# A clustered-attention, soft-MoE and PReLU kernel: the feed-forward's first steps in another order, another dispatch of the second batch, one more weight unit fetched in attention

## The chip, the cores and the metric

The kernel runs on one core of a Trainium2 chip. The metric is the device time of one execution in microseconds; three executions of the kernel before were timed, and one more was profiled.

## The reference

Three layers stand one behind the other, in float32. Attention has 2 batches of 8 heads, 768 tokens and 64 features: each query and key is assigned to one of 16 centroids of its head, and a query sees only the keys of its own cluster. The result, 1536 tokens of 512 features, goes through a soft mixture of 8 experts with 4 slots each, and then through a feed-forward with PReLU.

```python
mask = q_assign[:, :, :, None] == k_assign[:, :, None, :]
scores = np.where(mask, scale * np.matmul(q, k.transpose(0, 1, 3, 2)), -1e9)
attn = np.exp(scores - np.max(scores, axis=-1, keepdims=True))
x = np.matmul(attn / (np.sum(attn, axis=-1, keepdims=True) + 1e-09), v)   # then (1536, 512)
logits = x @ phi                                                          # (1536, 32)
d = np.exp(logits - logits.max(0, keepdims=True)); d /= d.sum(0, keepdims=True) + 1e-09
slot_input = (d.T @ x).reshape(E, S_per_e, D)
slot_out[e] = np.maximum(slot_input[e] @ w1[e], 0.0) @ w2[e]              # for each expert e
c = np.exp(logits - logits.max(1, keepdims=True)); c /= c.sum(1, keepdims=True) + 1e-09
h = (c @ slot_out) @ w_in                                                 # d_ff = 2048
out = (np.maximum(h, 0.0) + alpha * np.minimum(h, 0.0)) @ w_out
```

## The kernel before

The order of the instructions on each engine is the order in which the program issues them; nothing re-orders them later. In attention that order comes from a table. Every step of every head is an event with a due time, `add(key, step, ...)`, where a head has six units of time, `s0 = 6 * h`; the events are sorted by their due times and each is issued as soon as the steps that it needs have been issued. The due times are entries of `TABLE`. Its field `ha` holds counts of filler matmuls of the start (`heat`: products that nobody reads), `hb`, `hn` and `wk` those of other places, and `w` the list of expert weights that are fetched while attention runs.

Weights come in units of 1 MiB. Each expert has four, two of `w1` and two of `w2`, so there are 32. Nineteen of them are fetched in attention, into a ring of 18 tiles (`r`, the pool `wr`, which the operands of the heads share) and into the tiles of attention's operands as these come free (`a`, `b`, `c`). After attention three more go into the pool `we`, and the others follow as the experts release the ring (`more_w`). All these transfers, and the heads' operands, are issued by one engine, SP (SyncE), in program order; an entry of that queue that has to wait for its tile holds those behind it.

The feed-forward's weights are words of 64 bits that are turned into float32 high and low parts on the chip. `w_in` is prepared in attention (`win_word`, `win_bits`, `win_sum`, `win_store`): its first 512 columns stay in the chip, and three quarters go to DRAM and come back with `win_back(1)` to `win_back(3)` on the same queue. `w_out` is loaded by `load_o` and prepared in the feed-forward.

After the last head come, in program order: the dispatch of the second batch (`dispatch(1, 0)` to `dispatch(1, 2)`: maximum over the tokens for each slot, exponential, sums, the product with the tokens), the slots' inputs `siT`, eight experts with the combination's steps `comb_step` between, and the slot outputs `so`, `sob`, `soT`. There is one factor for each batch, because each batch had a maximum of its own.

The feed-forward begins with the string `ff` of `TABLE`. Each word is a step: `W0` to `W3` are 16 matmuls each that multiply the slot outputs by a quarter of w_in (`w_prime`; W0 is written to the PSUM tile `Wq`, W1 to W3 to `Wr`), `p0` to `p3` split the first 128 columns of W0's result into high and low part (`w_base`), and `c1` copies the rest out of `Wr` (`take`), which `P` and `Q` split later. `m` is a matmul pair of the hidden layer (`hidden_mm`), `h`, `g`, `H`, `L` are the PReLU and its split on ScalarE, VectorE, ScalarE and VectorE, `o n.t` is three matmuls of output tile t (`outp`). `x` loads w_out, and `w`, `b`, `r`, `s`, `l` turn one of its column blocks into high and low part: `w` begins with two ScalarE steps, `s` is a ScalarE step, `l` is on POOL. The output tiles 5 and 4 have the same PSUM as `Wq` and `Wr`. Behind the string a loop goes over the hidden blocks 3 to 31; in it, `hidden_mm` and the PReLU of a later block stand between the output matmuls. The last block's tiles are copied out of PSUM, by ScalarE and VectorE in turn, and stored.

In the rows below `unit_wr` is a tile of the ring, whatever is in it; `misc`, `s`, `L`, `ot`, `hp` and `ob` are PSUM tiles; `in_w` is the experts' weights, `in_w_in` and `in_w_out` those of the feed-forward, `wsp` the three stored quarters. `L596` is a filler matmul after attention, `L237` one at the start.

Of the kernel before, what the change touches and what calls it, by code (L numbers as in the profile page):

```python
# [16 lines left out]
P = 128  # L17
S = 768
NH = 16
# [14 lines left out]
    t_lo=-3, z_lo=-18.25, md=(0, 1), ld=(-0.95, 4.1, 2.65, 1.15, 0.95, -0.05), e_sum=9.9,
    e_rt=10.61, e_lg0=5.9, e_lg1=5.7, e_xnat=-5.95, lead=4, s1=-0.85, av=1.65, sum=7.9, rt=7.01,
    lg0=-1.6, lg1=3.5, xnat=9.45, t_sum=9.1, t_rt=-0.2, t_lg0=24.05, t_lg1=21.1, t_xnat=31.3,
    u_sum=11.4, u_rt=11.7, u_lg0=11.35, u_lg1=9.2, u_xnat=9.3, mr0=-1.25, mr1=0.9, mr2=1.6,
    z_mr0=-6.75, z_mr1=-3.4, z_mr2=-1.5, ph0=-21.35, ph1=-7.6, oh=-7.05, lo=-1.2, v=-8.6,
    raw=-23.6, sims=-17.5, nat=-13.65, p0=-14.55, p1=-13.85, p2=-11.25, oht=-9.85, hq0=-7.8,
    hq1=-6.3, hk=-6.25, lq0=-13.7, lq1=-8.75, lk=-4.3, y_v=-6.6, y_sims=-25.9, y_nat=-11.65,  # L40
    y_p0=-11.45, y_p1=-7.85, y_p2=-13.55, y_oht=-6.45, y_hq0=-7.9, y_hq1=-4.95, y_hk=0.45,
    y_lq0=-8.7, y_lq1=-9.05, y_lk=-13.85, y_rn=-2.8, rest=-7.65, x0=-5.7, x2=60.95, d0=0.1,
    d1=0.25, d2=2.45, nl0=-26.65, nl1=-35.25, nl2=-14.8, nl3=-10.8, nl4=-5.4, nl5=-3.7,
    no0=-16.25, no1=-13.55, no2=-10.7, no3=-3.1, no4=-2.15, no5=0.35, nr0=1, nr1=1.5, nr2=1.3,
    nr3=3.2, nrn=1.6, dz=(1.35, 13.35), do0=0.65, do1=2.6, do2=2.95, do3=3.3, do5=4.05, sp=15,
# [28 lines left out]
def clustered_attention_soft_moe_prelu_ffn(  # L74
# [43 lines left out]
    const = tp(ctx, "const", 1)  # L118
    ear = tp(early, "ear", 1)
# [548 lines left out]
    def dispatch(b, i, si=None, between=lambda: None):  # L668
# [690 lines left out]
```

## Time and profile before

| | us |
|---|---|
| three timed runs: median (lowest to highest) | 482.44 (481.29 to 483.86) |
| the profiled execution's time | 481.76 |
| its span, first to last instruction | 479.9 |
| TensorE busy | 446.9 (93%) |
| VectorE, ScalarE, POOL busy | 313.8, 288.7, 233.7 |

The span lies inside the execution's time; 1.86 us lie around it. TensorE is the busiest engine, but fillers count as busy. In the rows, a time in brackets is how long the engine had been idle before the instruction, and behind the arrow stands what released it.

### The profile page before, as it was taken

The page shows a single profiled execution, that of the slowest core. Times are in us where ns is not written, and L with a number is a line of the kernel's source. Part 1 is how long each engine was busy: PE and PEld are TensorE (multiplying, and loading weights), DVE is VectorE, ACT ScalarE, POOL GpSimd, SP SyncE. Part 2 cuts the span into 40 slices and gives each one's busy share as a digit, 9 for nine tenths or more (in the row PEclk, how much of TensorE's full clock was granted, in tenths as well). Part 3 has the DMA queues.
Part 4 walks back from the last instruction along what each step waited for, and adds up shares of the span by engine and source line. Part 5 has one row for each costly group of instructions (what it writes and reads, how often), then busy time and mean ns, then how long its engine had stood idle before and what let it go on. Part 6 is the DMA issues. An engine that isn't in the chain of part 4 may idle for free.

```text
span 479.9 us, 8319 instructions
## 1 busy us (share of the span) xinstructions
PE 446.9 (93%) x3002; PEld 301.2 (63%) x3002; DVE 313.8 (65%) x530; ACT 288.7 (60%) x532; POOL 233.7 (49%) x277
## 2 busy tenths in 40 slices
PE   4898999899999999999998889969999999999996
PEld 3674655555565656665644454447688888888885
DVE  3777978858779876786741641345899985444442
ACT  4668687577868757767645211347999855343341
POOL 4715788879988886998977000023433330000000
PEclk9999999999999999999999999997999999999999
DMA  8794974566877857668768899998120003000003
GB/s 320 210 294 137 317 243 128 138 199 193 258 232 227 244 176 235 195 221 260 214 202 279 308 331 397 398 415 325 71 93 13 2 0 131 1 0 1 0 0 133
DMA packets 35182, 90.51 MB, mean 189 GB/s; under 512 B 5250, under 2 KB 5590, under 8 KB 34756
## 3 DMA queue, kind: packets, MB, share of 16 engines
q1 hardware_dynamic: 34852, 89.86, 56.4%
q8 instruction: 24, 0.39, 0.3%
q14 instruction: 18, 0.15, 0.1%
q10 hardware_dynamic: 288, 0.11, 0.1%
HBM read 69.57 MB, written 6.33 MB: 158 GB/s over the span
## 4 chain that ended last, share of the span: by engine, by line
PE 64%; DVE 13%; DMA 7%; issue 6%; ACT 6%; POOL 3%; SPq 0%; ACTq 0%; POOLq 0%; DVEq 0%
PE s L552 9%; PE ot L580 9%; PE ob L1247 9%; PE ob L1249 9%; PE ob L1248 9%; PE s L484 5%; DVE cs L491 4%; DMA unit_wr<-wsp 4%; PE hp L1211 2%; PE s L1033 2%; PE L L1051 2%; POOL ss L568 2%; ACT pt L555 2%; PE ot L237 2%; DMA B<-unit_wr 1%
## 5 line engine op out<-in xcount | busy, mean ns | idle before, releaser
L568 POOL TENSOR_TENSOR ss<-ss,pt 128x384 f32<-128x384 f32 x150 | 145.5, 1002 | 18.3 <-PE ot L580 17.2
L491 DVE TENSOR_REDUCE cs<-s 128x1 f32<-128x768 f32 x93 | 88.6, 953 | 39.2 <-PE s L484 38.7
L555 ACT ACTIVATE pt<-s 128x384 f32<-128x384 f32 x160 | 69.8, 488 | 52.6 <-PE s L552 48.9
L552 PE MATMUL s<-A,B 97*128 97x384 f32 (+1 forms) x384 | 94.0, 365 | 4.0 <-ACT pt L555 3.5
L552 PEld LDWEIGHTS s<-A,B 97*128 97x128 f32 (+1 forms) x384 | 63.3, 190 | 32.3 <-issue 16.2
L1247 PE MATMUL ob<-unit_wr,gh 128*128 128x512 f32 x192 | 76.8, 400 | 0.0
L1248 PE MATMUL ob<-unit_wr,gh 128*128 128x512 f32 x192 | 76.4, 398 | 0.2 <-POOL unit_wr L1141 0.2
L1249 PE MATMUL ob<-unit_wr,gl 128*128 128x512 f32 x192 | 76.5, 399 | 0.0
L1141 POOL TENSOR_TENSOR unit_wr<-unit_wr 128x256 fp32r<-128x256 f32 x32 | 26.4, 844 | 89.8 <-DMA unit_wr<-wsp 49.2
L580 PE MATMUL ot<-pt,raw_v 128*64 128x384 f32 x320 | 61.6, 497 | 0.0
L484 PE MATMUL s<-B,A 96*128 96x384 f32 x192 | 53.4, 360 | 5.8 <-DVE cs L491 3.3
L1233 DVE SCALAR_TENSOR_TENSOR g<-hp,sal,hs 128x768 f32<-128x768 f32 (+1 forms) x34 | 32.8, 968 | 30.8 <-ACT hs L1231 30.7
L1231 ACT ACTIVATE hs<-hp,sgn 128x768 f32<-128x768 f32 (+1 forms) x34 | 29.1, 861 | 32.8 <-PE hp L1211 32.6
L484 PEld LDWEIGHTS s<-B,A 96*128 96x128 f32 x192 | 32.4, 189 | 18.1 <-DVE cs L491 13.4
L1249 PEld LDWEIGHTS ob<-unit_wr,gl 128*128 128x128 f32 x192 | 36.4, 190 | 8.9
L1248 PEld LDWEIGHTS ob<-unit_wr,gh 128*128 128x128 f32 x192 | 36.5, 190 | 8.5 <-POOL unit_wr L1141 1.1
L1247 PEld LDWEIGHTS ob<-unit_wr,gh 128*128 128x128 f32 x192 | 36.4, 190 | 7.6 <-issue 0.4
L1237 DVE TENSOR_TENSOR gl<-g,gh 128x768 fp32r<-128x768 f32 (+1 forms) x34 | 30.9, 911 | 15.1 <-ACT gh L1235 14.9
L1235 ACT ACTIVATE gh<-g 128x768 fp32r<-128x768 f32 (+1 forms) x34 | 27.4, 806 | 17.6 <-DVE g L1233 17.4
L580 PEld LDWEIGHTS ot<-pt,raw_v 128*64 128x64 f32 x320 | 20.0, 136 | 23.7 <-issue 23.0
L237 PE MATMUL ot<-cs,identb 128*128 128x256 bf16 x155 | 20.7, 289 | 5.3 <-DVE least L216 5.3
L725 POOL TENSOR_TENSOR unit_wr<-unit_wr 128x256 uint32<-128x256 uint32 x32 | 22.6, 727 | 4.8 <-DVE unit_wr L718 4.8
(182 smaller groups left out, 607.7 us busy)
## 6 DMA issues: line engine op xcount, KB each, us to landing
unit_wr<-in_w SPq DMA_DIRECT2D x28, 512.0 KB
unit_wr<-in_w SPq DMA_DIRECT2D x11, 1024.0 KB
unit_wr<-in_w_in SPq DMA_DIRECT2D x16, 512.0 KB
unit_wr<-in_w_out SPq DMA_DIRECT2D x5, 1024.0 KB
unit_wr<-in_qT SPq DMA_DIRECT2D x8, 384.0 KB
unit_wr<-in_kT SPq DMA_DIRECT2D x8, 384.0 KB
unit_wr<-in_qn SPq DMA_DIRECT2D x8, 384.0 KB
unit_wr<-in_kn SPq DMA_DIRECT2D x8, 384.0 KB
```

The source lines that it names most:

```text
L237: pe.matmul(heats[0][:, :256], identb, ident.bitcast(BF16), start=True, stop=True)
L484: pe.matmul(ps[hf], a[:96, c * P:c * P + P], b[:96, hf * 384:hf * 384 + 384], start=True, stop=True,)
L491: dve.tensor_reduce(m, t, axis=AX.XY, op=ALU.max, negate=True)
L552: pe.matmul(ps[:, :384], b[:, c * P:c * P + P], a[:, hs], start=(i == 0), stop=(i == 1))
L555: act.activation(e[:, hs], ps[:, :384], AF.Exp, scale=0.125)
L568: (pool if h < T["sp"] else dve).tensor_tensor(ss[h][:, hs], ss[h][:, hs], sme[h, c][:, hs], op=ALU.add)
L580: pe.matmul(ot[h][hf * 64:hf * 64 + 64, :], v[:, c, par * 64:par * 64 + 64], e[:, hf * 384:hf * 384 + 384], start=(c == 0), stop=(c == 5),)
L1233: dve.scalar_tensor_tensor(g, hv, sal[:, f:f + 1], hs, op0=ALU.mult, op1=ALU.max)
L1237: dve.tensor_tensor(gl, g, gh.bitcast(F32), op=ALU.subtract)
L1247: pe.matmul(ob[t], gh[:, c], wh(f), start=(f == 0), stop=False)
L1248: pe.matmul(ob[t], gh[:, c], wlo(f), start=False, stop=False)
L1249: pe.matmul(ob[t], gl[:, c], wh(f), start=False, stop=(f == 15))
```

## The change

The change has eight parts. (1) The table's due times and filler counts are other numbers: of `ha` the first goes from 22 to 15 and the second from 1 to 11, and `w` has 20 units rather than 19, with a pool `wg` of one tile for the new one; the tile of `c` is filled when the last head is done, where it was the last but one. (2) The string `ff` is re-ordered. (3) Of w_in's returning quarters the second is issued before the second half of w_out's first load. (4) The dispatch of the second batch takes the maximum of its own batch alone, computes both factors from the two maxima, and accumulates `si` with the factor in one VectorE instruction; the two `xnat` products of the last head are put off into the dispatch; `G` is loaded early; `siT` is made from one `si` by half as many matmuls, and `Gr` is gone. (5) The roots' sums are in an SBUF tile `rs` rather than in the logits' PSUM tile, and the tile `lt` is now `tr`. (6) The combination's steps come after experts 3, 5 and 6 rather than 4, 5 and 6, and the fillers in the last expert are (4, 2) rather than (4, 6). (7) VectorE's half of the slot outputs has a tile of its own, `sob2`. (8) The last output tile is copied and stored in two halves, by ScalarE and VectorE.

```diff
-    f0=3, rp=(), ha=(22, 1, 36, 13, 0, 7), hb=(0, 0, 8, 5, 3, 0),
+    f0=3, rp=(), ha=(15, 11, 34, 11, 0, 6), hb=(0, 0, 0, 8, 0, 2),
     ff="""
-        b0 r0 w1 W0 p0 s0 b1 l0 W1 m0 x2 c0 W2 h0.0 h0.1 g0.0 p1 g0.1 H0.0 H0.1 W3 c1 L0.0 p2 r1
-        L0.1 s1 o0.0 l1 x3 o0.1 m1 o0.2 o0.3 o0.4 o0.5 h1.0 h1.1 g1.0 g1.1 p3 H1.0 H1.1 L1.0 L1.1
+        x2 b0 r0 W0 p0 m0 s0 h0.0 h0.1 W1 l0 c0 p1 g0.0 g0.1 H0.0 H0.1 L0.0 L0.1 W2 w1 p2 b1 r1 o0.0
+        m1 s1 o0.1 x3 W3 o0.2 o0.3 h1.0 o0.4 l1 h1.1 g1.0 c1 g1.1 o0.5 m2 p3 H1.0 H1.1 L1.0 w2 L1.1
...
-    w7=(4, 6), wc=(6, 3, 8), pipe=6, ws=16, wk=(0, 0, 3, 6, 3, 3, 3, 0, 8, 3, 0, 0),
+    w7=(4, 2), wc=(6, 3, 8), pipe=6, ws=16, wk=(0, 0, 3, 6, 3, 3, 3, 0, 8, 3, 0, 0),
...
-            o = cor.tile([P, 384], F32, name="osb", bufs=2)
+            o = cor.tile([P, 384], F32, name="osb")
...
-        e = zz[h][:, 384:390]
+        e = cor.tile([P, 6], F32, name="rs")
...
-            t = cor.tile([P, 192], F32, name="lt") if h % 8 else L
+            t = cor.tile([P, 192], F32, name="tr") if h % 8 else L
...
-        ps = misc()
+        ps = misc() if h < NH - 1 else ps1.tile([P, 2, 512], F32, name="s1")[:, 0]
...
+        if h == NH - 1:
+            rest.extend(todo)
+        else:
+            for f in todo:
+                f()
...
-            for g in range(b + 1):
-                pe.transpose(ps[:1, g * P:g * P + P], ml[:, g:g + 1], ident)
+            pe.transpose(ps[:1, :P], ml[:, b:b + 1], ident)
+            between()
...
+            between()
             dve.tensor_copy(ml[:, b:b + 1], ps[:, :1])
             act.activation(dT, L, AF.Exp, bias=ml[:, b:b + 1], accum_out=zs[:, b:b + 1])
+            if b:
+                dve.tensor_tensor(rz, ml[:, :1], ml[:, 1:], op=ALU.min)
+                dve.tensor_tensor(fac, rz.to_broadcast([P, 2]), ml, op=ALU.subtract)
+                act.activation(fac, fac, AF.Exp)
...
-            dve.tensor_copy(si or dsp["si"], ps[:, :256])
+            si = dsp["si"]
+            if b == 0:
+                dve.tensor_copy(si, ps[:, :256])
+            else:
+                dve.scalar_tensor_tensor(
+                    si, ps[:, :256], fac[:, 1:2], si, op0=ALU.mult, op1=ALU.add
+                )
...
+    warm(wk[5])
+    dispatch(1, 0, rest[0])
+    warm(wk[6])
+    dispatch(1, 1, rest[1])
     core.close()
     cp = tp(ctx, "cp", 1, side="right")
-    G = cp.tile([P, P], F32, name="G")
-    sp.dma_start(out=G, in_=grp)
     refill("e", 3)
     more_w(3, lf["e"])
...
-        for b in range(2):
-            dve.tensor_scalar(Gr[:, b], G[:, :32], fac[:, b:b + 1], None, op0=ALU.mult)
+        dve.tensor_scalar(dsp["si"], dsp["si"], fac[:, 0:1], None, op0=ALU.mult)
...
-            for b in range(2):
-                pe.matmul(
-                    ps[:, k * 32:k * 32 + 32], SI[b][l0:l0 + 64, k * P:k * P + P],
-                    Gr[l0:l0 + 64, b], start=(b == 0), stop=(b == 1),
-                )
+            pe.matmul(
+                ps[:, k * 32:k * 32 + 32], dsp["si"][l0:l0 + 64, k * P:k * P + P],
+                G[l0:l0 + 64, :32], start=True, stop=True,
+            )
...
-        if 4 <= e < 7:
-            comb_step(e - 3)
+        if e in (3, 5, 6):
+            comb_step((e - 1) // 2 if e < 6 else 3)
...
                 win_back(1)
+                win_back(2)
                 sp.dma_start(out=u[:, 1], in_=src[:, f1])
-                win_back(2)
                 win_back(3)
...
+    sob2 = cp.tile([P, 256], F32, name="sob")
     act.copy(sob[:, :256], so[:, :256])
-    dve.tensor_copy(sob[:, 256:], so[:, 256:])
+    dve.tensor_copy(sob2, so[:, 256:])
...
+            if n == 31 and t == 5:
+                act.copy(o[:, :256], ob[t][:, :256])
+                dve.tensor_copy(o[:, 256:], ob[t][:, 256:])
+                act.dma_start(out=out[r0:r0 + P, :256], in_=o[:, :256])
+                sp.dma_start(out=out[r0:r0 + P, 256:], in_=o[:, 256:])
+                return
```

Three places show how the instructions move. A row is a line of its own kernel, the operation, the tile written, the tiles read, the shape; x2 means two in a row.

The first place is VectorE from the last head's logits to the maximum of the second batch. Before, with the two `xnat` products (L659, L663) ahead of the maximum (L671):

```order
L644 TENSOR_TENSOR lt<-L,sm 128x192
L646 TENSOR_TENSOR unit_wr<-unit_wr,lt 128x192
L659 TENSOR_TENSOR unit_wr<-misc_3306,rin 128x4x64
L663 TENSOR_TENSOR unit_wr<-misc_3306,rin 128x2x64
L671 TENSOR_REDUCE ml<-unit_wr 128x1
L675 TENSOR_REDUCE unit_wr<-misc_3332 1x32
L685 COPY ml<-misc_3340 128x1
L687 STREAM_TRANSPOSE unit_wr<-unit_wr 128x192
L943 TENSOR_TENSOR fac<-ml 128x2
```

VectorE of the changed kernel, at the same place:

```order
L650 TENSOR_TENSOR tr<-L,sm 128x192
L652 TENSOR_TENSOR unit_wr<-unit_wr,tr 128x192
L686 TENSOR_REDUCE ml<-unit_wr 128x1
L666 TENSOR_TENSOR unit_wr<-s_3333,rin 128x4x64
L690 TENSOR_REDUCE unit_wr<-misc_3341 1x32
L670 TENSOR_TENSOR unit_wr<-s_3333,rin 128x2x64
L701 COPY ml<-misc_3348 128x1
L704 TENSOR_TENSOR rz<-ml 128x1
L705 TENSOR_TENSOR fac<-rz,ml 128x2
L707 STREAM_TRANSPOSE unit_wr<-unit_wr 128x192
```

The maximum (L686) now stands directly behind the logits, each `xnat` product between two steps that wait for TensorE, and the factors ahead of the transposition.

The second place is ScalarE from the slot outputs' copy (L1150) on. Before, the two `w` steps of w_out's second column block (the second L707 and L708) stand ahead of p0 (the first L1194), and c1's copy (L1267) ahead of the second pair of `h` steps (L1231):

```order
L1150 COPY unit_wr<-L 128x256
L707 ACTIVATE unit_wr<-unit_wr 128x512
L708 ACTIVATE unit_wr<-unit_wr,s_3401 128x512
L707 ACTIVATE unit_wr<-unit_wr 128x512
L708 ACTIVATE unit_wr<-unit_wr,s_3401 128x512
L1194 ACTIVATE unit_wr<-ob_3762 32x128 x2
L1134 ACTIVATE unit_wr<-unit_wr 128x512
L1231 ACTIVATE hs<-hp,sgn 128x384 x2
L1194 ACTIVATE unit_wr<-unit_wr 32x128 x2
L1235 ACTIVATE gh<-g 128x384 x2
L1267 COPY unit_wr<-ob_3763 128x384
```

ScalarE of the changed kernel, where L1290 is c1's copy and L1248 the `h` steps:

```order
L1166 COPY unit_wr<-L 128x256
L733 ACTIVATE unit_wr<-unit_wr 128x512
L734 ACTIVATE unit_wr<-unit_wr,s_3417 128x512
L1211 ACTIVATE unit_wr<-ob_3774 32x128 x2
L1149 ACTIVATE unit_wr<-unit_wr 128x512
L1248 ACTIVATE hs<-hp,sgn 128x384 x2
L1211 ACTIVATE unit_wr<-unit_wr 32x128 x2
L1252 ACTIVATE gh<-g 128x384 x2
L733 ACTIVATE unit_wr<-unit_wr 128x512
L734 ACTIVATE unit_wr<-unit_wr,s_3417 128x512
...
L1248 ACTIVATE hs<-hp,sgn 128x384 x2
L1290 COPY unit_wr<-ob_3775 128x384
```

The `w` steps of the second block have gone behind the first PReLU, and c1's copy behind the second pair of `h` steps.

The third place is TensorE at the ramp's first matmuls. Before, W0 and W1 (the tiles ob_3762 and ob_3763), m0 (hp), W2 and W3, and the first matmul of an output tile; each of these matmuls is two instructions in the trace:

```order
L1174 MATMUL ob_3762<-unit_wr 32x128 x16
L1174 MATMUL ob_3763<-unit_wr 32x128 x16
L1211 MATMUL hp<-unit_wr 128x384 x2
L1174 MATMUL ob_3763<-unit_wr 32x128 x32
L1247 MATMUL ob_3873<-unit_wr,gh 128x512
```

TensorE of the changed kernel:

```order
L1191 MATMUL ob_3774<-unit_wr 32x128 x16
L1228 MATMUL hp<-unit_wr 128x384 x2
L1191 MATMUL ob_3775<-unit_wr 32x128 x32
L1264 MATMUL ob_3867<-unit_wr,gh 128x512
L1265 MATMUL ob_3867<-unit_wr,gh 128x512
L1266 MATMUL ob_3867<-unit_wr,gl 128x512
L1228 MATMUL hp<-unit_wr 128x384 x2
L1264 MATMUL ob_3875<-unit_wr,gh 128x512
L1265 MATMUL ob_3875<-unit_wr,gh 128x512
L1266 MATMUL ob_3875<-unit_wr,gl 128x512
L1191 MATMUL ob_3775<-unit_wr 32x128 x16
```

m0 follows W0 at once, W1 and W2 come behind it, and W3 behind the first two output tiles.

## Rows read from the trace of the kernel before

**Rows 1.** Windows by stage: length, busy us by engine, clock, DMA share, GB/s.
```profile
40.00:268.00 228.00, 215.58 (x1431) 130.74 (x1426) 166.04 (x295) 159.27 (x328) 187.69 (x208) 1.00 0.72 223
...
282.00:315.00 33.00, 31.14 (x409) 14.07 (x407) 8.32 (x24) 6.80 (x16) 0.00 (x0) 1.00 1.01 377
...
315.00:345.00 30.00, 24.53 (x210) 18.72 (x209) 20.16 (x34) 22.84 (x44) 9.88 (x14) 0.89 0.63 253
...
345.00:476.00 131.00, 131.00 (x575) 107.05 (x573) 83.81 (x97) 73.11 (x101) 19.20 (x24) 1.00 0.09 34
```

**Rows 2.** The page, span in 40 slices: DMA engines' busy share in tenths.
```profile
DMA  8794974566877857668768899998120003000003
```

**Rows 3.** Windows of three us: dispatch's start, experts, ramp; columns as before.
```profile
270.00:273.00 3.00, 2.42 (x20) 0.91 (x19) 2.48 (x11) 0.48 (x1) 0.59 (x1) 1.00 0.43 153
...
288.00:291.00 3.00, 3.00 (x52) 1.42 (x45) 0.45 (x1) 0.47 (x1) 0.00 (x0) 1.00 1.04 406
...
324.00:327.00 3.00, 3.00 (x35) 2.32 (x28) 1.78 (x4) 1.84 (x6) 0.72 (x2) 0.50 1.02 406
```

**Rows 4.** Timeline, start: time, us, engine, operation, out, in, count, [idle before, releaser].
```profile
5.30 4.25 PE L237 MATMUL ot<-cs,identb 128*128 128x256 bf16 x22 [5.30 <-DVE least L216]
...
6.72 0.54 DVE L248 TENSOR_SCALAR unit_wr<-unit_wr,cs 128x64 f32<-128x64 f32 x2
...
9.70 0.29 DVE L256 COPY CB<-misc 128x128 f32<-128x128 f32 x1 [2.44 <-PE misc L254]
...
11.58 0.55 PE L355 MATMUL misc<-cs,unit_wr 128*128 128x128 f32 x3 [0.46 <-ACT unit_wr L349]
```

**Rows 5.** Timeline of the second batch's dispatch.
```profile
273.02 0.54 PE L636 MATMUL L<-osb,phz 128*32 128x96 f32 x16 [0.59 <-DVE rin L621]
...
273.67 0.36 DVE L644 TENSOR_TENSOR lt<-L,sm 128x192 f32<-128x192 f32 x1 [0.39 <-PE L L636]
...
274.36 0.42 DVE L659 TENSOR_TENSOR unit_wr<-misc,rin 128x256 f32<-128x256 f32 x1
...
274.70 0.28 DVE L663 TENSOR_TENSOR unit_wr<-misc,rin 128x128 f32<-128x128 f32 x1
...
275.60 0.41 DVE L675 TENSOR_REDUCE unit_wr<-misc 1x32 f32<-1x256 f32 x1 [0.36 <-PE misc L674]
```

**Rows 6.** The chain of waits, in attention and at siT's matmuls: start, us, what.
```profile
121.35 5.86 DMA B<-unit_wr
...
280.40 1.55 PE misc L967 x16
```

**Rows 7.** Timeline of the experts' end.
```profile
305.68 0.68 PE L1007 MATMUL misc<-unit_wr 128*128 128x128 f32 x6 [0.41 <-DVE unit_wr L999]
...
312.11 0.83 PE L596 MATMUL s<-cs,identb 128*128 128x256 bf16 x6
...
313.72 1.06 PE L1051 MATMUL L<-unit_wr,hT 128*32 128x512 f32 x8 [0.78 <-DMA unit_wr<-in_w]
```

**Rows 8.** Timeline of the feed-forward's ramp.
```profile
316.75 1.96 PE L1174 MATMUL ob<-unit_wr 128*32 128x128 f32 x64
...
318.78 0.66 ACT L707 ACTIVATE unit_wr<-unit_wr 128x512 uint32<-128x512 uint32 x1 [2.34 <-DMA unit_wr<-in_w_out]
...
321.26 0.59 PE L1211 MATMUL hp<-unit_wr 128*128 128x384 f32 x2 [2.56 <-ACT unit_wr L1134]
...
323.75 1.94 PE L1174 MATMUL ob<-unit_wr 128*32 128x128 f32 x32 [0.89 <-DMA unit_wr<-wsp]
...
325.76 0.48 ACT L1267 COPY unit_wr<-ob 128x384 f32<-128x384 f32 x1 [1.08 <-PE ob L1174]
...
329.22 1.05 ACT L1231 ACTIVATE hs<-hp,sgn 128x384 f32<-128x384 f32 x2 [1.67 <-PE hp L1211]
```

**Rows 9.** Timeline: the slot outputs' second half, and the last copy.
```profile
315.25 0.42 DVE L1151 COPY unit_wr<-L 128x256 f32<-128x256 f32 x1 [4.30 <-ACT unit_wr L1150]
...
476.18 0.69 DVE L1252 COPY o<-ob 128x512 f32<-128x512 f32 x1 [0.71 <-PE ob L1249]
```

More of the change, by code (lines that the diff above doesn't have):

```diff
@@ L33 @@
-    """,
[L34 to L45, printed above, removed]
@@ new lines @@
+        m1 s1 o0.1 x3 W3 o0.2 o0.3 h1.0 o0.4 l1 h1.1 g1.0 c1 g1.1 o0.5 m2 p3 H1.0 H1.1 L1.0 w2 L1.1
+        b2 h2 w3 g2 H2 r2 s2 o1.0 o1.1 l2 o1.2 L2 o1.3 o1.4 m3 h3 w4 g3 b3 H3 L3 r3 P0 Q0 s3 x4 l3
+        b4 o1.5 o2.0 r4 o2.1 o2.2 o2.3 m4 h4 s4 w5 o2.4 g4 b5 r5 H4 w6 L4 l4 o2.5
+    """,
+    t_lo=-4.3, z_lo=-20.25, md=(0, 1), ld=(-1.35, 4.1, 2.65, 1.15, 0.95, -0.05), e_sum=9.6,
+    e_rt=11.11, e_lg0=5.25, e_lg1=5.9, e_xnat=-4.95, lead=4, s1=-0.85, av=1.65, sum=7.9,
+    rt=0.61, lg0=-0.8, lg1=3.25, xnat=9.65, t_sum=6.8, t_rt=1.7, t_lg0=18.85, t_lg1=21.6,
@@ new lines @@
+    d0=0.1, d1=0.95, d2=2.85, nl0=-26.1, nl1=-39, nl2=-18.5, nl3=-10.8, nl4=-6.9, nl5=-2,
+    no0=-15.65, no1=-14.3, no2=-10.35, no3=-3.05, no4=-2.2, no5=0.35, nr0=1, nr1=1.7, nr2=1,
+    nr3=3, nrn=0.5, dz=(1.35, 13.15), do0=0.65, do1=2.6, do2=2.95, do3=3.4, do5=4.15, sp=15,
+    w7=(4, 2), wc=(6, 3, 8), pipe=6, ws=16, wk=(0, 0, 3, 6, 3, 3, 3, 0, 8, 3, 0, 0),
+    dl=(-36.95, -44.2, 0.85, 2.35, 14.35, 19.75, 26.05, 32, 33.55, 44.05, 45.35, 57.5, 61.9,
+        68.15, 73.6, 80.9),
+    w=(
+        ('r', -0.85, 5.25),
+        ('r', 4.25, 6.5),
+        ('r', 11.8, 14.55),
+        ('r', 27.25, 29.75),
+        ('r', 41.85, 43.2),
+        ('r', 46.15, 53.65),
+        ('r', 50.3, 51),
+        ('g', 59.4, 62.4),
+        ('r', 60.95, 67.85),
+        ('r', 65.05, 66.55),
+        ('r', 71.1, 83),
+        ('r', 72.9, 73.15),
+        ('r', 79.45, 79.6),
+        ('r', 83.2, 87.5),
+        ('r', 92.04, 102.99),
+        ('a', 94.95, 97.85),
+        ('r', 96.8, 111.95),
+        ('a', 97.5, 97.5),
+        ('b', 99.1, 99.15),
+        ('c', 106.5, 108),
@@ L118, in clustered_attention_soft_moe_prelu_ffn @@
     const = tp(ctx, "const", 1)
+    wg = tp(late, "wg", 1)
     ear = tp(early, "ear", 1)
@@ L190, in load_rest @@
             sp.dma_start(out=alp, in_=alpha)
+            sp.dma_start(out=G, in_=grp)
     wts = {}
@@ L1156, in clustered_attention_soft_moe_prelu_ffn @@
         pe.matmul(
-            ps[:, k * 32:k * 32 + 32], sob[:, k * P:k * P + P], G[:, :32], start=True, stop=True
+            ps[:, k * 32:k * 32 + 32], (sob, sob2)[k // 2][:, k % 2 * P:k % 2 * P + P], G[:, :32],
+            start=True, stop=True,
         )
```

76 lines of the change are left out of this document (27 added, 49 removed).

## The prediction

> **What bounds the kernel now.** I read the stage windows first [rows 1]. From 345 to 476 us TensorE is busy 131.00 of 131.00 us: the loop of the feed-forward hides everything else, and no edit can win there but at the last instruction. Attention from 40 to 268 us leaves TensorE 228.00 − 215.58 = 12.4 us idle. The expert stage leaves 33.00 − 31.14 = 1.9, and the feed-forward's ramp, 315 to 345 us, 30.00 − 24.53 = 5.5, at a mean granted clock of 0.89. So a gain has to come out of these gaps, or out of filler matmuls and latency between small steps that count as busy.
>
> The DMA queue is the second thing to see. The DMA slices stand at 8 to 9 from the 22nd slice to the 28th (12 us each) [rows 2], which is the end of attention, the experts and two thirds of the ramp. In three-us windows the rate is 406 GB/s where the queue is full, and 153 at 270 to 273 us [rows 3], where the operands of attention have just come free and little is queued. The ramp's window 324 to 327 is granted 0.50, the 1.2 GHz level [rows 3].
>
> **Start of the kernel.** 22 fillers take 4.25 us, 0.193 each, from 5.30 to 9.55 us, and the centroids' transpose stands behind them; its operand is done at 6.72 + 0.54 = 7.26, and CB begins at 9.70 [rows 4]. Fifteen fillers free the transpose 7 × 0.193 = 1.35 us earlier. But eleven fillers now stand ahead of the transpose at 11.58, where one stood, and that one waits only 0.46 us for ScalarE [rows 4]: ten more at 0.193 are 1.9 us against 1.35 + 0.46 = 1.8 of room. The bound that pays is 0 to −1.35. I take −0.3, near the small end, since the 11.58 row is the one that the next VectorE steps need.
>
> **Attention.** The due times change for most steps, one more megabyte of weights is fetched before the end, and G's 64 KB load is early. Fourteen heads of work and 12.4 us of idle time [rows 1] are 0.9 us a head. No row says which due time is better, so I take 0, bounds ±1.5 us (about 0.1 us a head). The extra megabyte is 1.05 MB at 406 GB/s [rows 3] = 2.6 us of transfer in a stage where the queue isn't full; it is hidden there, and costs up to 2.6 us if it delays the last head's operands.
>
> **Dispatch of the second batch.** Today the two logit and normalising chains go through one PSUM tile: TensorE waits 0.59 us for `rin` before the last head's logit matmuls, and VectorE then waits 0.39 us for them [rows 5]. With the roots in `rs` the matmuls run beside VectorE's four small steps, and the 0.39 goes. The two `xnat` products, 0.42 + 0.28 = 0.70 us, stand ahead of the maximum [rows 5]; afterwards they stand in the waits behind it. One such wait is 0.36 us before the minimum [rows 5], so of the 0.42 some 0.06 sticks out, and two small factor steps on VectorE now lie in ScalarE's exponential. The minimum reads 128 elements rather than 256: of its 0.41 us about 0.1 goes. That is 0.39 + 0.70 − 0.06 + 0.1, about 1.1; I take 0.9, because TensorE's fillers and the reloads between are of one length and don't all move. The scaling of `si` by the first factor (256 columns) replaces the two Gr products, and the accumulation replaces a copy of 0.42 us: equal. The siT matmuls are eight pieces rather than sixteen, which took 1.55 us [rows 6]; the experts start on the first half, so between 0.39 and 0.78, I take 0.5. **Dispatch −1.4**, bounds −0.9 to −1.7.
>
> **Experts.** The combination's first part is moved from after expert 4 to after expert 3. At its last step TensorE waits 0.41 us for VectorE [rows 7]; with the steps an expert earlier, this wait is gone. At the end the last weight unit is late: TensorE fills from 312.11 and starts the last half at 313.72 with a wait of 0.78 on the DMA [rows 7], so the unit is 313.72 − 312.11 = 1.6 us late. With the gains above TensorE would want it at 312.11 − 1.4 − 0.41 = 310.3. One unit less is fetched after attention (12, not 13): 2.6 us, so it lands at 313.72 − 2.6 = 311.1. If the hole at 270 to 273 is also filled, since the first loads no longer stand behind G's, another (406 − 153) / 406 × 3 = 1.9 us. The last half thus begins between 310.3 and 311.1, 2.6 to 3.4 us earlier, of which 1.4 is the dispatch. **Experts −1.6**, bounds −0.4 (the wait alone) to −2.3.
>
> **Feed-forward's ramp.** On ScalarE the word steps of the second w_out column block stand ahead of `p0`, and the first of them waits 2.34 us for its DMA until 318.78 [rows 8]; TensorE, which has done W0 and W1 at 316.75 + 1.96 = 318.71, waits 2.56 us and starts m0 at 321.26 [rows 8]. The new order puts p0 right behind W0, and behind nothing that needs a DMA. W0 alone ends at 316.75 + 0.98 = 317.73. p0 began after two word steps (0.66 us each, 318.78 + 1.32 = 320.1), and m0 followed 1.16 us later; so m0 is at 317.73 + 1.16 = 318.9, 2.4 earlier. TensorE's wait of 0.89 us for the third returning quarter [rows 8] goes too: its transfer is 2.6 us earlier with the missing unit, and W3 is later in the string. Against this, TensorE is idle for the 1.16 us between W0 and m0, where W1 stood. And o0.4 needs c1's copy (the tile `ob4` is Wr). ScalarE does that copy, 0.48 us, now behind two h1 steps of 1.05 us together [rows 8], where it was ahead of them: 1.5 us in which TensorE holds, and with it every later outp and hidden_mm. That makes −2.4 − 0.9 + 1.2 + 1.5 = −0.6. The outp matmuls that fell in the 0.50 stretch took longer [rows 3]; I add −0.4 for a shorter stretch. **Ramp −1.0**, bounds +1.5 (nothing regained but the new wait) to −3.3 (both waits gone and no new one).
>
> **Tail and the slot outputs.** `sob2` gives VectorE's half of the copy a tile of its own. Today that half, 0.42 us, starts only when ScalarE's ends [rows 9], and a tile they share would explain it: then the edit is worth about 0.4 us. The last output tile is copied in two halves; VectorE's whole copy takes 0.69 us [rows 9], halves side by side 0.42, one after another 0.84, and the last transfer is half as large. I take 0 for both, bounds ±0.4.
>
> The Trainium skill speaks against these two edits. Its page PSUM — Partial Sum Buffer, section PSUM bank collisions raise a hardware error, says that two engines must not touch one bank and 32-partition quadrant at once, two readers included, so a scheduler puts a dependency between them. By that rule both pairs of halves stay one behind the other: nothing won at `sob2`, and 0.84 against 0.69 us at the last copy. By the row alone, a shared tile, the sum would be 0.7 us better. The row shows the wait and can't say which of the two it is.
>
> **Sum.** −0.3 + 0 − 1.4 − 1.6 − 1.0 + 0 = −4.3. The profiled execution took 481.76 us, so 477.5; it lay 0.68 below the median of the three runs, 482.44, so the median comes out at **478.1**.
>
> **Rivals.** About 0.5%, 2.4 us, is what a measurement can tell from no change: faster is under 480.0, slower over 484.9.
> (a) As summed, with each term near its value: 476.2 to 480.0, chance 0.45.
> (b) The ramp keeps all that it wins: the c1 wait falls in other idle time and the clock stays up. Ramp −3.3: 482.44 − 0.3 − 1.4 − 1.6 − 3.3 = 475.8. For it: TensorE has 5.5 us idle there. Chance 0.17.
> (c) The new due times also fill idle time of attention, 0.2 us a head over 14 heads, −2.8: 475.3. Chance 0.10.
> (d) The DMA sets the experts' end whatever the dispatch does: the queue is as late as before since the last operands' pool, `wc`, is now filled only after the last head. Then dispatch and experts give nothing, and 482.44 − 0.3 − 1.0 = 481.1, same. For it: the last unit was late already [rows 7]. Chance 0.12.
> (e) TensorE's idle time between W0 and o0.0 lengthens the stretch at 0.50: each us in it costs half a us. With the 1.16 us idle, 1.5 us at c1 and a stretch 3 us longer, ramp +2.0 instead of −1.0: 481.1, same. Chance 0.08. The Trainium skill's page TensorE: Matmul & The Clock Gate, section What's actually happening, has the throttled state as the default and activity as what releases it; the trace agrees that the fall to 0.50 follows TensorE's idle time at 318.78 to 321.26.
> (f) Slower: weight loads put ahead of the heads' operands on the one queue. The chain of waits has a stretch of 5.86 us that ends on the DMA of the operand B [rows 6], so an operand lands just in time there. If every head from the second on loses 0.6 us behind a load of 1.05 MB, 14 × 0.6 = 8.4 against −4.3: 486.5. It decides from (4.3 + 2.4) / 14 = 0.48 us a head. Against it: TensorE is 95% busy in attention. Chance 0.08.
>
> Faster 0.45 + 0.17 + 0.10 = 0.72, same 0.20, slower 0.08. The range, 474.0 to 482.2, holds (a), (d) and (e), and (b) and (c) but for their best ends; it leaves out (f).
>
> **What would show it.** After: the last head's logit matmuls with no wait on `rin`; from them to the first expert matmul 1.4 us less than before; no wait of 0.41 us in the combination; the last half of the experts with a DMA wait well under 1.6 us. In the ramp: no DMA wait on ScalarE ahead of p0, m0 some 2 us nearer to W0, W3 with no DMA wait, and a wait of o0.4 on ScalarE's c1 copy. The last two copies one behind the other. From the ramp on, TensorE without a gap, as now. I am wrong if attention's end moves by over 1.5 us either way, if the last unit lands no earlier against the end of attention, or if the ramp is longer than 30 us.

## The result, and the profile after

The changed kernel takes 478.02 us (median of 22 runs, 474.82 to 482.98), the kernel before 482.00 (22 runs, 478.72 to 485.22). The ratio is 0.9918, 95% interval 0.9892 to 0.9944: faster by 4.0 us, where the prediction had 478.1 against 482.44. The sum was right; not all of its parts were, and the trace shows it. Here and below the ratios leave out the few executions over 1.5% above the fastest of their kernel, and the medians count every one.

The profiled execution took 480.53 us with a span of 478.0, so it lies 2.5 us above its median. I cut both spans at four marks: the last pair of attention matmuls, the first expert matmul, the end of the last expert half, the last matmul. Of the kernel before, in the timeline, the first two (the others are in [rows 7, 9]: 313.72 + 1.06 = 314.78, and the last matmul starts at 475.74):

```profile
270.59 0.87 PE L580 MATMUL ot<-pt,raw_v 128*64 128x384 f32 x4
...
281.88 0.42 PE L1033 MATMUL s<-unit_wr,siT 128*32 128x256 f32 x4
```

And the timeline after, from the last attention matmuls to the experts, and the experts' end:

```profile
274.13 0.87 PE L586 MATMUL ot<-pt,raw_v 128*64 128x384 f32 x4
...
276.13 0.54 PE L642 MATMUL L<-osb,phz 128*32 128x96 f32 x16 [0.23 <-DVE tr L621]
...
277.72 0.35 DVE L686 TENSOR_REDUCE ml<-unit_wr 128x1 f32<-128x192 f32 x1
277.99 0.41 DVE L666 TENSOR_TENSOR unit_wr<-s,rin 128x256 f32<-128x256 f32 x1
...
278.43 0.28 DVE L690 TENSOR_REDUCE unit_wr<-misc 1x32 f32<-1x128 f32 x1
...
284.19 1.93 PE L1048 MATMUL s<-unit_wr,siT 128*32 128x256 f32 x32 [0.30 <-DVE siT L986]
...
314.18 0.39 PE L602 MATMUL s<-cs,identb 128*128 128x256 bf16 x2
...
314.50 1.06 PE L1066 MATMUL L<-unit_wr,hT 128*32 128x512 f32 x8
```

| us | before | after | difference | predicted |
|---|---|---|---|---|
| to the last attention matmuls | 270.59 | 274.13 | +3.5 (at the medians +1.4) | −0.3 |
| dispatch, to the first expert matmul | 11.29 | 10.06 | −1.2 | −1.4 |
| experts | 32.90 | 31.37 | −1.5 | −1.6 |
| to the last matmul (ramp and loop) | 160.96 | 158.30 | −2.7 | −1.0 |
| from the last matmul to the end | 4.16 | 4.14 | 0.0 | 0 |

Behind attention the change wins 5.4 us and not the 4.0 that were forecast there. Since the medians differ by 4.0, attention and the start have lost about 1.4 us at the medians, if the stages behind are of one length in every execution; in this one they lost 3.5, which is over the 1.5 that the prediction named as a sign that it is wrong.

In the dispatch the reader sees the steps that were forecast: the logits wait for the transposition and no longer for `rin` [rows 5], the maximum stands ahead of the `xnat` product, and the minimum takes 0.28 us where it took 0.41. Of the 1.23 us, 0.43 are won ahead of the last head's logit matmuls (2.43 us behind the last attention matmuls, now 2.00) and 0.80 behind them, where the prediction had looked for 1.4. The last expert half has no wait on a DMA.

The ramp after, in the timeline:

```profile
317.53 1.08 PE L1191 MATMUL ob<-unit_wr 128*32 128x128 f32 x32
...
320.01 0.59 PE L1228 MATMUL hp<-unit_wr 128*128 128x384 f32 x2 [1.40 <-ACT unit_wr L1149]
...
322.96 0.50 PE L1264 MATMUL ob<-unit_wr,gh 128*128 128x512 f32 x1 [0.47 <-ACT gh L1252]
...
325.06 1.08 PE L1191 MATMUL ob<-unit_wr 128*32 128x128 f32 x32
...
328.38 0.48 ACT L1290 COPY unit_wr<-ob 128x384 f32<-128x384 f32 x1
...
328.91 0.50 PE L1264 MATMUL ob<-unit_wr,gh 128*128 128x512 f32 x1 [1.18 <-ACT unit_wr L1290]
```

m0 starts 4.45 us behind the experts' end, where it was 6.48 (321.26 − 314.78); 1.40 us of idle time stand between W0 and m0 (1.16 forecast), W3 waits for no DMA, and o0.4 waits 1.18 us for c1's copy (1.5 forecast). The window from 315 to 345 us is granted 1.00 throughout, where its mean was 0.89 [rows 1].

The waits of TensorE in the 36 us behind the experts' end, before:

```profile
PE hp L1211 <- ACT unit_wr L1134: 2.6, 1, 2.6
PE hp L1211 <- ACT unit_wr L1188: 1.0, 1, 1.0
PE ob L1174 <- DMA unit_wr<-wsp: 0.9, 1, 0.9
PE hp L1211 <- DVE g L1233: 0.8, 1, 0.8
PE ob L1248 <- POOL unit_wr L1141: 0.2, 1, 0.2
```

and after:

```profile
PE ob L1265 <- POOL unit_wr L1156: 1.6, 2, 1.2
PE hp L1228 <- ACT unit_wr L1149: 1.4, 1, 1.4
PE ob L1264 <- ACT unit_wr L1290: 1.2, 1, 1.2
PE hp L1228 <- ACT unit_wr L1205: 0.9, 1, 0.9
PE ob L1264 <- ACT gh L1252: 0.5, 1, 0.5
```

The sums are 5.5 and 5.6 us: the change moves the waits and doesn't shorten them. What it takes away is the stretch at the low clock. Before, the windows from 324 to 327 us [rows 3] and from 327 to 330 were granted 0.50 and 0.56, with TensorE busy for all of their 3.00 us; 0.50 × 3.00 + 0.44 × 3.00 = 2.8 us is an estimate of what the full clock would have saved there, and the ramp is shorter by 2.7.

The last two copies are one behind the other, and so are the slot outputs':

```profile
316.04 0.42 DVE L1167 COPY sob<-L 128x256 f32<-128x256 f32 x1 [2.91 <-ACT unit_wr L1166]
...
474.29 0.37 ACT L1271 COPY o<-ob 128x256 f32<-128x256 f32 x1
...
474.70 0.42 DVE L1272 COPY o<-ob 128x256 f32<-128x256 f32 x1 [1.12 <-ACT o L1271]
```

VectorE's half has a tile of its own now and waits for ScalarE all the same, so the shared tile was not what held it. The rule that the prediction cites would hold it; no run has the two halves in two banks.

Where attention loses is in the chain of waits, the timeline and two windows of 12 us:

```profile
149.47 8.69 DMA B<-unit_wr
```

```profile
158.29 1.30 PE L558 MATMUL s<-A,B 128*128 128x384 f32 x3 [2.00 <-DMA B<-unit_wr]
```

```profile
144.00:156.00 12.00, 11.25 (x82) 7.20 (x78) 11.68 (x23) 10.34 (x21) 10.13 (x12) 1.00 0.90 261
156.00:168.00 12.00, 10.00 (x61) 5.91 (x63) 6.75 (x15) 6.67 (x15) 5.79 (x8) 0.72 0.66 174
```

One head's operand B is issued at 149.47 and is there only at 158.2; TensorE waits 2.00 us, and then the granted clock of the next 12 us is 0.72. Up to there the execution is level with the one before (the same matmul stands at 144.28 and 144.44). On SP, a load of keys and half a weight unit stand ahead of that head's operand transfers:

```profile
146.73 0.33 SPq L174 DMA_DIRECT2D unit_wr<-in_kn  x1
...
147.10 0.43 SPq L209 DMA_DIRECT2D unit_wr<-in_w  x1
...
147.64 0.50 SPq L106 DMA_DIRECT2D A<-lowq  x1
...
149.47 1.34 SPq L106 DMA_DIRECT2D B<-unit_wr  x1
```

This is the mechanism of rival (f), at one head and not at fourteen.

### The profile page after: what moved, and what is told of

Its sections match the earlier page's. It is cut to its first block, busy times and chain, and to the rows that moved or that the text cites. A ratio compares the mean times of both kernels' runs of the same rounds, so it can differ in the third digit from the quotient of the medians.

```text
span 478.0 us, 8314 instructions
## 1 busy us (share of the span) xinstructions
PE 446.4 (93%) x2988; PEld 299.8 (63%) x2988; DVE 313.9 (66%) x530; ACT 286.8 (60%) x533; POOL 233.3 (49%) x277
## 4 chain that ended last, share of the span: by engine, by line
PE 73%; DVE 12%; ACT 6%; issue 4%; DMA 3%; POOL 1%; ACTq 0%; SPq 0%; POOLq 0%; DVEq 0%
PE s L558 11%; PE ot L586 11%; PE ob L1265 9%; PE ob L1266 8%; PE ob L1264 8%; PE s L490 7%; DVE cs L497 5%; PE ot L243 4%; PE s L1048 3%; PE L L1066 3%; PE hp L1228 2%; DMA B<-unit_wr 2%; PE misc L350 1%; ACT pt L561 1%; PE misc L661 1%
## 5 line engine op out<-in xcount | busy, mean ns | idle before, releaser
L586 PE MATMUL ot<-pt,raw_v 128*64 128x384 f32 x320 | 62.9, 506 | 0.0
L1248 ACT ACTIVATE hs<-hp,sgn 128x768 f32<-128x768 f32 (+1 forms) x34 | 29.1, 861 | 30.5 <-PE hp L1228 30.3
L490 PEld LDWEIGHTS s<-B,A 96*128 96x128 f32 x192 | 33.7, 196 | 18.1 <-DVE cs L497 12.7
```

The lines of the kernel that those rows point to most:

```text
L490: pe.matmul(ps[hf], a[:96, c * P:c * P + P], b[:96, hf * 384:hf * 384 + 384], start=True, stop=True,)
L586: pe.matmul(ot[h][hf * 64:hf * 64 + 64, :], v[:, c, par * 64:par * 64 + 64], e[:, hf * 384:hf * 384 + 384], start=(c == 0), stop=(c == 5),)
```

## The experiments

All runs in one table: median us (number of runs), ratio to the kernel before on the same chip with its interval, then the dispatch, the experts and the time from their end to the last matmul in the profiled execution.

| run | median (runs) | ratio, 95% interval | dispatch | experts | ramp and loop |
|---|---|---|---|---|---|
| 1: load behind the operands | 475.62 (6) | 0.9860 (0.9818 to 0.9902) | 10.06 | 31.38 | 158.86 |
| 2: old table | 479.49 (12) | 0.9938 (0.9910 to 0.9966) | 10.07 | 31.36 | 158.35 |
| 3: old string | 480.63 (12) | 0.9961 (0.9927 to 0.9995) | 10.06 | 31.38 | 158.04 |
| 4: c1 and r2 earlier | 481.30 (12) | 0.9955 (0.9918 to 0.9991) | 10.06 | 31.39 | 159.46 |
| 5: as it is | 478.77 (10) | 0.9907 (0.9869 to 0.9944) | 10.06 | 31.38 | 158.87 |
| 6: run 1, 19 units | 475.13 (4) | 0.9839 (0.9797 to 0.9881) | 10.05 | 31.38 | 158.34 |
| 7: run 6, G late | 473.92 (4) | 0.9838 (0.9780 to 0.9896) | 10.05 | 31.38 | 158.31 |
| 8: run 1, old string and order | 474.68 (4) | 0.9826 (0.9783 to 0.9868) | 10.06 | 31.38 | 156.01 |
| 9: run 6, old string and order | 472.65 (6) | 0.9806 (0.9770 to 0.9842) | 10.06 | 31.37 | 156.71 |
| 10: before, experts' edits | 481.55 (10) | 0.9984 (0.9950 to 1.0018) | 11.28 | 31.92 | 160.19 |
| 11: run 1, xnat early | 474.46 (1) | | 10.47 | 31.37 | 158.31 |
| 12: before, tiles of part 5 | 479.02 (12) | 0.9937 (0.9906 to 0.9967) | 11.06 | 31.96 | 156.82 |

**Run 1: the load behind the operands.**

```diff
-        ('r', 46.15, 53.65),
+        ('r', 48.6, 53.65),
```

> The changed kernel with one due time moved: the first half of one weight unit, 0.5 MB, is issued behind one head's operand transfers instead of ahead of them (46.15 becomes 48.6 in the list w). Theory 1: the changed kernel's attention ends late because this load and the one before it delay the operand B, for which TensorE waits 2.0 us at 156 to 158 us, and then runs a stretch at a lower granted clock (0.72 from 156 to 168 us). Then that wait is gone or under 0.5 us, the clock of that stretch is 1.00, and the median is 475.0 to 476.8 against 478.0. Rival: the late operand belongs to that one profiled execution alone, and the median is 478.0 within 1 us.

The waits of TensorE in attention, of this run:

```profile
PE s L558 <- DMA B<-unit_wr: 0.6, 1, 0.6
```

The wait fell from 2.0 to 0.6 us (just over the 0.5 that was expected), the window from 156 to 168 us is granted 1.00, and the median is 475.62, inside what Theory 1 gave. The spread is smaller as well, in 6 executions against 22: 474.5 to 477.9 against 474.8 to 483.0. The place of half a megabyte on the queue costs the changed kernel some 2.4 us. The intervals of the two ratios still touch (0.9892 and 0.9902), but the profiles agree: with the load ahead of the operands (the first profile, runs 3, 4 and 5) TensorE waits 2.0, 3.7, 2.4 and 3.2 us for B, with the load behind them (runs 1, 6, 7, 8, 9 and 11) never more than 0.8.

**Run 5: the changed kernel once more.**

> The changed kernel as it is, once more, with a profile of its own. Theory: the wait of TensorE for the operand B at 156 us is there in this execution too, 1.5 to 4 us, and its size sets the spread of the times; the stages behind attention are the same as in the first profile within 0.2 us (10.06 us from the last attention matmul to the first expert matmul, 31.4 us of experts, 158.3 from there to the last matmul). Rival: the wait is absent, so the first profile was an accident.

```profile
PE s L558 <- DMA B<-unit_wr: 3.2, 2, 2.3
```

The wait is there again, 3.2 us in two places, and the ten times reach from 474.5 to 484.4. But here the clock stayed at 1.00, and the execution took 477.0: of the loss, the wait is one part and the clock behind it another, which comes and goes (0.72, 0.72 and 0.86 from 156 to 168 us in the first profile and runs 3 and 4). So the size of the wait alone doesn't set the time. The ramp, 158.87, is 0.6 us longer than in the first profile, where 0.2 was expected; the seven profiles with the new string as it is give 158.30 to 158.87, and smaller differences are not read below. The start is a second source of spread: the window from 12 to 24 us was granted 0.88 in the first profile, 0.84 to 0.87 in runs 1, 3 and 8, and 1.00 in the six other runs with the new fillers. With the old fillers (before, runs 2, 10 and 12) it was 1.00 each time. Where the clock is up, the first scores come at 18.5 to 18.9 us, with the old fillers at 19.2 to 20.2: the start wins something like the 0.3 that was forecast, or more. In the four with a lower clock they come at 18.9 to 19.4, and the first attention product is 2 us later than in the six (last section). The due times changed with the fillers, so this is not the fillers' effect alone.

**Run 2: the old table.** The attention part of `TABLE`, with its fillers and 19 units, is that of the kernel before; `ff` and `w7` are the new ones.

> The changed kernel with the attention part of the old table: its due times, fillers and 19 weight units; the feed-forward's string, the dispatch, the combination and the rest stay changed. Theory 1: the new due times cost time in attention (+1.4 us in the median, 3.5 in the profiled execution) and all the gain lies behind it; then attention ends as in the kernel before, the last weight unit is late again by some of its 1.6 us, and the median is 475.5 to 478.0. Rival: the new due times are part of the gain, and the median is 479.0 or more.

The rival was right: 479.49, and the experts take 31.36 us, so no unit is late again. With the new code, the old due times are 3.9 us slower than the new ones with the load moved (run 1), and 0.7 to 1.5 slower than the changed kernel itself (run 5 and the result), which the intervals don't tell from no difference. So the new due times are no loss but for that load. What makes the old ones slow under the new code was asked in run 12.

**Run 12: the tiles of part 5 alone, in the kernel before.**

```diff
-            o = cor.tile([P, 384], F32, name="osb", bufs=2)
+            o = cor.tile([P, 384], F32, name="osb")
...
-        e = zz[h][:, 384:390]
+        e = cor.tile([P, 6], F32, name="rs")
...
-            t = cor.tile([P, 192], F32, name="lt") if h % 8 else L
+            t = cor.tile([P, 192], F32, name="tr") if h % 8 else L
```

The first line of the diff, one buffer of `osb` instead of two, belongs to part 5 as well.

> The kernel before with the fifth part of the change alone: the roots' sums in the SBUF tile rs, the logits' product in the tile tr instead of lt, and one osb buffer instead of two. Theory: the run with the old table and the new code lost 3 to 4 us in attention against the first run because these shared tiles make a head wait for the one before it under the old due times; attention ends 1.5 to 4 us later than in the kernel before, median 484 to 486.5. Rival: the tiles cost nothing under the old due times, and the old table lost against the new one by its due times alone; median 482.3 to 483.7, like the kernel before.

Both medians failed: the kernel got faster, 479.02 against 481.51. The theory's step in attention came true. With the old due times and the new tiles the last attention matmuls stand at 275.18 us (here) and 275.69 (run 2), with the old due times and the old tiles at 270.59 (before) and 272.36 (run 10), so 2.8 to 5.1 us later. The tiles by themselves make attention slow under the old due times, which answers what run 2 left open; which of the three does it was not tested. But the stages behind attention are shorter by 0.2, 0.9 and 4.1 us. On SP, the kernel before had

```profile
271.52 0.33 SPq L931 DMA_DIRECT2D G<-in_grp  x1
271.90 1.50 SPq L203 DMA_DIRECT2D unit_we<-in_w  x3
```

and this run has

```profile
264.75 1.12 SPq L931 DMA_DIRECT2D G<-in_grp  x1
...
273.04 4.47 SPq L203 DMA_DIRECT2D unit_we<-in_w  x3
...
275.18 0.87 PE L580 MATMUL ot<-pt,raw_v 128*64 128x384 f32 x4
```

G's load stands ahead of the three expert loads. Before, it waited 11.0 us for the matmuls of line 580 and went out when the last of them had ended (270.59 + 0.87), with the three loads behind it, the first 1.3 us behind the start of the last attention matmuls. With the fewer core tiles, G's load waits for nothing. The first of the three loads is then issued 2.1 us ahead of the last attention matmuls; the other two follow 1.4 and 1.9 us behind them, 0.5 us earlier than before. In the ramp, ScalarE waits 0.67 us for w_out's second column block, where it waited 2.34 [rows 8], and no window there is granted less than 1.00. That the earlier issue of these loads is the whole cause is not shown: run 7 holds them again, and nothing is late.

**Runs 6 and 7: the twentieth unit, and G.** Run 6 takes `('g', 59.4, 62.4)` out of run 1's list. Run 7 is run 6 with

```diff
-    G = const.tile([P, P], F32, name="G")
...
-            sp.dma_start(out=G, in_=grp)
...
+    G = cp.tile([P, P], F32, name="G")
+    sp.dma_start(out=G, in_=grp)
     refill("e", 3)
```

> The first run's kernel (the load moved behind the operands) without the twentieth unit: the entry g is taken out of the list w, so that thirteen units are fetched after attention, as before. The prediction had 2.6 us of earlier arrival from this unit: by it, the last expert half waits again and the experts take 32.2 to 33.0 us instead of 31.4. Theory now: the loads are early enough without it, because they no longer stand behind G's; experts 31.4, and the ramp within 0.5 of 158.9.

> The same with 19 units, and G again in the pool that takes the place of attention's core tiles, its load directly ahead of the first three expert loads behind attention. Theory: G's load waits for the last head's tiles and holds the expert loads on SP by 2 us or more; the last unit is late again by 1.0 to 2.0 us, the experts take 32.2 to 33.2 us, and the ramp is longer by 0.5 to 2.5, so the median is 477.5 to 479.5. Rival: G's place costs nothing and the gain of the experts comes from the combination's earlier step and fewer fillers; experts 31.4 to 31.8.

The unit is worth nothing behind attention: 31.38 and 158.34 without it. Run 7 holds the loads as was thought (the first is issued 1.3 us behind the last attention matmuls, in run 6 2.1 ahead), and still nothing behind attention is longer. So neither is the experts' gain by itself. On the queue it shows: w_out's first load, behind the experts' units on SP, is issued 14.67 us after the first expert matmul in run 6, 15.86 in run 7, and 18.01 before. There was room for the 1.2 us that G's place costs; what makes the queue earlier than before by the rest was not taken apart.

**Run 10: the experts' edits in the kernel before.** The combination after experts 3, 5 and 6, and `w7=(4, 2)`.

> The kernel before with one part of the change: the combination's steps after experts 3, 5 and 6, and fillers (4, 2) in the last expert. Theory: without the earlier loads the last unit still arrives 41.8 us behind the first load issued after attention, so the 0.41 us and the four fewer fillers turn into a longer wait on the DMA; experts 32.7 to 33.0 as before, median 481 to 483. Rival: these two edits are the experts' gain by themselves; experts 31.4 to 31.9, median 480 to 481.

```profile
314.49 1.07 PE L1051 MATMUL L<-unit_wr,hT 128*32 128x512 f32 x8 [0.48 <-DMA unit_wr<-in_w]
```

The rival was nearly right: the experts take 31.92, 1.0 less, with 0.48 us of waiting left. In the time nothing is clear (0.9950 to 1.0018): in the ramp TensorE still waits 2.6 us for the operand behind w_out's block and 1.1 us for a returning quarter.

**Run 11: the xnat products early.** In run 1's kernel they run where they are defined, for the last head as well.

> The first run's kernel with the last head's two xnat products made at their old place, ahead of the second batch's maximum, instead of in the waits behind it. By the prediction's term (0.70 us less 0.06 that sticks out) the time from the last attention matmul to the first expert matmul grows from 10.06 to 10.6 to 10.8 us. Rival: the products stood in time that VectorE had anyway, and it stays under 10.3.

The dispatch is 10.47, by 0.41 longer: between the two, and two thirds of the 0.64 that the prediction had for it.

**Runs 3, 8 and 9: the string and the order of the quarters.** Run 3 is the changed kernel with the old `ff`; run 8 is run 1 with the old `ff` and the old order of `win_back`; run 9 is run 6 with both. So run 3 differs from run 8, behind attention, in the order of the quarters alone.

> The changed kernel with the old feed-forward string, all else changed. Theory 1, from the two traces: from the experts' end to the last matmul the change saved 2.7 us, nearly all by the order of the string; the median is 480.2 to 481.2, and the stretch at 0.50 is back in the ramp. Rival, as predicted: the string is worth 1.0, since part of the 2.7 is the earlier transfers; the median is 478.5 to 479.5.

> The first run's kernel with the old string and the old order of the returning quarters. Theory: the ramp's gain of 2.7 us comes from transfers that are early, not from the string or the order of the quarters; from the experts' end to the last matmul 158.0 to 159.2 us, median 475.3 to 476.5. Rival: the two orders matter together; 160.5 or more, median 477.5 or more.

> The first run's kernel with the three edits that gave nothing or lost undone: 19 units, the old string, the old order of the returning quarters. Theory: the stages add up: attention as in the run with nineteen units, experts 31.4, and from their end to the last matmul 156.0 us; median 472 to 473.5, below both kernels and all runs so far. Rival: with thirteen units to fetch behind attention the second column block of w_out is late for the old string again, 158 or more, median 474.5 or more.

The median of run 3 fits Theory 1, but its ramp doesn't: it is not longer (158.04), and the time went into attention, where B was waited for 3.7 us. Of Theory 1 a low stretch did come back in the ramp (0.60 and 0.83 in the windows from 324 to 330 us). The rival was wrong too. Run 8 then has the shortest ramp of all, 156.0, under the 158.0 of its theory. What parts runs 3 and 8 is ScalarE ahead of p0. In run 3:

```profile
321.75 0.66 ACT L733 ACTIVATE unit_wr<-unit_wr 128x512 uint32<-128x512 uint32 x1 [1.99 <-DMA unit_wr<-in_w_out]
```

In run 8 this step doesn't wait for the DMA. The new order of the quarters puts w_out's second block behind the second quarter, and the old string, which needs the block ahead of p0, waits for it again: 2.0 us of ramp. The waits of TensorE in the 36 us behind the experts' end, of run 8, with the old string and the old order:

```profile
PE hp L1228 <- DVE g L1250: 1.0, 1, 1.0
PE hp L1228 <- ACT unit_wr L1205: 1.0, 1, 1.0
PE hp L1228 <- ACT unit_wr L1149: 0.5, 1, 0.5
PE ob L1265 <- POOL unit_wr L1156: 0.2, 1, 0.2
PE ob L1191 <- DMA unit_wr<-wsp: 0.2, 1, 0.2
```

2.9 us against the 5.6 of the changed kernel; the ramps of run 1 and run 8 differ by 2.85. The new string brings the waits for c1 and for POOL's low part, and a longer idle time between W0 and m0. The old one loses where its transfers are late, and the new order of the quarters is enough to make them late. So the 2.85 belong to the string and the order together: with the new order the old string gives 158.04 (run 3), the new one 158.30 to 158.87. The new string with the old order was not run. Run 9 puts together what the runs left standing, 472.65 us, as its theory had it; its ramp, 156.71, is 0.7 longer than the theory's, its rival's 158 was wrong. It is faster than both kernels, by 10.3 us than the one before.

**Run 4: c1, s1 and r2 moved in the new string.**

```diff
-        m1 s1 o0.1 x3 W3 o0.2 o0.3 h1.0 o0.4 l1 h1.1 g1.0 c1 g1.1 o0.5 m2 ...
-        b2 h2 w3 g2 H2 r2 s2 ...
+        m1 o0.1 x3 W3 c1 s1 o0.2 o0.3 h1.0 o0.4 l1 h1.1 g1.0 g1.1 o0.5 m2 ...
+        b2 h2 w3 r2 g2 s2 H2 ...
```

> The changed kernel with three steps of its string moved: c1 and then s1 directly behind W3, and r2 ahead of g2, s2 ahead of H2. Theory: TensorE's wait of 1.18 us for c1's copy goes, and its wait of 1.6 us for the low part of the third column block shrinks to about 0.6; the median is 475.5 to 476.3. Rival: ScalarE and VectorE are the bound of the ramp, so that the wait turns up at the next steps (the hidden block 2 or 3), and the median is 478.0 within 0.7.

The waits for c1 and for POOL's low part are gone, but the ramp is longer than in the changed kernel, 159.46. In the timeline:

```profile
339.27 0.92 PE L1228 MATMUL hp<-unit_wr 128*128 128x384 f32 x2 [2.00 <-ACT unit_wr L1205]
```

m4 waits 2.0 us for ScalarE, where it waited 0.93, and the window from 339 to 342 us is granted 0.57. The rival was right in kind: the wait turned up at a later step, though at block 4 and not at 2 or 3. The median of 481.3 is outside what either gave; it has attention's spread in it as well (B was waited for 2.4 us).

## Why the prediction was right, and where it was not

**The sum, 478.1, was right because two errors cancel**: the stages behind attention gave 5.4 us and not 4.0, and attention and the start lost 1.4 us at the medians where −0.3 was forecast. That the total came out within 0.1 us is luck.

**Dispatch, −1.4: right** in size (−1.2) and in its steps; the part of the xnat products was 0.41 of the 0.64 (run 11, one execution).

**Experts, −1.6: right in size, wrong in its largest cause.** The unit less behind attention, 2.6 us of transfer, is worth nothing here (run 6). In the trace the 1.5 are three things of about that sum: the wait of 0.78 us on the DMA, the 0.41 us in the combination, and four fillers (0.83 − 0.39 = 0.44 us). The edits of part 6 give 1.0 by themselves (run 10), the tiles of part 5 give 0.9 by themselves (run 12), and the whole change 1.5. That G's load held the first loads was read rightly, and the tiles of part 5 alone free it (run 12); but the last unit is on time with G late as well (run 7), so this is not what the experts' gain hangs on once the rest is changed. Why it is on time there stays open.

**Ramp, −1.0: the step that failed.** The prediction set the old waits against the new ones, −0.6, and gave the low stretch of the clock −0.4. The forecast terms were seen in the trace: m0 earlier by 2.0 (2.4 forecast), W3's wait gone, 1.40 between W0 and m0, 1.18 at c1. But there was one more, 1.6 us for POOL's low part, and the sum of the waits came out at +0.1 and not −0.6. The stretch, sized at 0.4, is the term that was far too small: by the estimate above it is some 2.8 us, and so the whole gain. Its second miss is that the earlier transfers by themselves are worth 4.1 us to the old string (run 12: waits of 3.8 us instead of 5.5, and no low stretch), so that the new string and the new order of the quarters then cost 2.9 together with 20 units (run 1 against 8) and 1.6 with 19 (run 6 against 9). With the new string m0 stands 4.45 us behind the experts' end in every run, early transfers or not; with the old string and order the ramp goes from 160.96 to 156.0 as they get earlier. The string is a remedy for a lateness that other parts of the change remove.

**Attention, 0 ± 1.5: inside its bounds at the medians, by a mechanism that was seen as a rival.** Rival (f) was priced as 0.6 us at each of fourteen heads. It was 2.0 to 3.7 us at one head or two, in three of the four profiles with a low clock behind it (the first, runs 3 to 5). That the loss stayed under 1.5 at the medians is luck as well: without that load's place attention and the start win some 1.7 us (run 1: 6.6 us in the medians, 4.9 of them behind attention).

**Tail and sob2, 0: right**, and the rule of the Trainium skill (PSUM — Partial Sum Buffer, section PSUM bank collisions raise a hardware error) fits: with two tiles the halves still stand one behind the other. Of rival (e), the stretch at 0.50 vanished in the ramp of this kernel; it is back, at 0.57, in run 4 behind a wait of 2.0 us, and at 0.60 in run 3 behind one of 2.2.

## What to carry to other kernels

When one part of a change makes transfers earlier and another re-orders work so that late transfers hurt less, test them apart: here the first made the second (the string and the order of the quarters) a loss of 1.6 to 2.9 us, which the sum didn't show. Two orders that go together are tested together and apart: the old string lost 2.0 us by the new order of the quarters alone. On one queue in program order, look for the large prefetch that stands directly ahead of a small transfer that somebody waits for; moving half a megabyte behind four small transfers was worth some 2.4 us, and the times spread less. And cut a trace by stages before reading any gain: a total that agrees can hold two errors.

## What was not expected

The granted clock differs between executions of one program. With the new fillers the window from 12 to 24 us was granted 0.84 to 0.88 in four of ten profiles and 1.00 in six, and the first attention product came at 40.9 to 41.7 us instead of 38.8 to 39.1. Run 9 with the old fillers was not tried.
